# A three-step conversion of 64-bit weights with its word in an output bank, and three GpSimd tasks moved, in a fused attention and feed-forward kernel

## The chip, the core and the metric

The kernel runs on one core of a Trainium2 chip. The core has five engines with queues of their own: TensorE (PE in the profile, with its weight loads as PEld), VectorE (DVE), ScalarE (ACT), GpSimd (POOL) and SyncE (SP), which here issues almost all DMAs. Each engine takes its instructions in the order in which the program lists them, and waits where an operand is not ready. The metric is the device time of the whole program in microseconds (us), from the first to the last instruction and what lies around it; lower is better.

## What is computed

Two stages follow each other. The first is attention in 4 batches of 8 heads, with 768 tokens of 64 channels a head; a query sees only keys whose hash of six sign bits is the same. The second is a feed-forward layer on the 3072 tokens, whose two weight matrices come as 64-bit floats.

```python
q_bits = (einsum('bhsd,dk->bhsk', q, proj) > 0)      # six bits of each query
k_bits = (einsum('bhsd,dk->bhsk', k, proj) > 0)
mask = q_bucket[:, :, :, None] == k_bucket[:, :, None, :]
scores = where(mask, scale * q @ k.T, -1e9)
attn = exp(scores - max(scores)); attn = attn / (sum(attn) + 1e-9)
x = (attn @ v).transpose(0, 2, 1, 3).reshape(3072, 512)
h = x @ w_in                                          # w_in 512 x 2048, float64
g = where(h >= 1, h, where(h <= -1, 0, (h + 1)**2 / 4))
y = (g @ w_out).astype(float32)                       # w_out 2048 x 512, float64
```

## The kernel before

**Units.** The attention of the 32 heads is cut into 384 units, 12 a head: two halves of 384 queries, times six blocks of 128 keys. Here "unit 9" counts within a head; an even head and the odd head behind it share a pair of q, k and v tiles. Unit g issues two score matmuls into one of four PSUM buffers `s` (lines 372 and 373), two exponentials on ScalarE (lines 381 and 386, a rounded `ph` and an exact copy) and, one unit later, their difference `pl` on VectorE, or on GpSimd in units 0, 3, 6 and 9 (line 39 is the helper of all subtractions). Four units later come the three product matmuls with the values (lines 405, 407, 409). They gather a half of the queries in one of two output banks: bank 0 (`o_137` in the order of instructions) from unit 4 to unit 9, bank 1 (`o_138`) from unit 10 to unit 3 of the next head. When a half is complete, ScalarE copies it out (line 415).

**Row maxima.** In every second unit two matmuls `smax` (line 311) compute scores of a later head, which VectorE reduces to row maxima (line 315). There is one `smax` buffer of two banks, so the next `smax` pair can start only when the reduction of the one before is done. When all six are there, GpSimd clamps them (`max_clamp`, lines 343 and 345), TensorE transposes them (`max_tr`, line 350), ScalarE copies them (line 355) and a DMA puts them into row 7 of the operand tile `t` (line 357), which the score matmuls of that head read.

**Operands of the next pair.** GpSimd casts and splits q and k in four quarters (`cast_h`, line 153, and `low_h`) in units 0 to 3 of an even head; `move` (line 164) copies parts between partitions by DMA. `bits_mm` (line 211) computes the hash bits in an output bank that is free at that moment, ScalarE and VectorE compare them (lines 217 and 222), GpSimd scales them (line 274).

**Weights.** `WeightSplit.steps` turns a block of 128 x 512 64-bit floats into 32-bit ones by their bits. Line 69 (ScalarE) squares the high word as a float, line 70 (VectorE) shifts the high word, lines 74, 78 and 82 (VectorE) add sign, low bits, and a zero where the value is too small. Twelve blocks of `w_in` start in the odd heads 3 to 25, twelve more blocks (four of `w_in`, eight of `w_out`) in the even heads 4 to 26, and eight of `w_out` in the feed-forward stage. So from head 3 to head 26 each head has one block; its steps are set by the numbers in `conv`, units counted from the start of the head:

```python
conv((2 * i + 3) * NU, wi_steps(i, nc.scalar), (0, 7, 9, 13, 15, 17, 19, 21))
conv((4 + 2 * n) * NU, first, (0, 7, 9, 13, 15, 16))
```

The order is written by hand: `at(g, fn)` puts a task behind the matmuls of unit g, and tasks of one unit go in the order in which they were registered, weights first. On VectorE a unit reads: reduction of the last `smax`, difference `pl` of the unit before, then tasks. The feed-forward stage (`ffn`) has its own tables.

Of the kernel before, what the change touches and what calls it, by code (L numbers as in the profile page):

```python
# [22 lines left out]
P = 128  # L23
# [11 lines left out]
WMIN2 = float(np.array([897 << 20], np.int32).view(np.float32)[0]) ** 2  # L35
# [6 lines left out]
class WeightSplit:  # L42
# [3 lines left out]
    def __init__(self, nc, pool, n):  # L46
        self.nc, self.pool, self.n = nc, pool, n
        sc = pool.tile([P, 2], I32, name="wsc", bufs=1)
        nc.vector.memset(sc[:, 0:1], -0x40000000)
        nc.vector.memset(sc[:, 1:2], 29)  # L50
        self.sc = sc

    def steps(self, src, shape, hi, lo, cp, stage=None, low=None, keep=None):
# [10 lines left out]
        def s1():  # L64
            raw = st["raw"]
            sq = st["sq"] = self.pool.tile([P, n], F32, name="wsq")
            a = st["a"] = self.pool.tile([P, n], I32, name="wa", bufs=1)
            high = raw[:, :, 1].bitcast(F32)
            nc.scalar.activation(out=sq, in_=high, func=AF.Square)
            nc.vector.tensor_scalar(out=a, in0=raw[:, :, 1], scalar1=0x07FFFFFF, scalar2=3,  # L70
                                    op0=ALU.bitwise_and, op1=ALU.logical_shift_left)

        def s2():
            nc.vector.scalar_tensor_tensor(out=st["a"], in0=st["raw"][:, :, 1], scalar=self.sc[:, 0:1],
                                           in1=st["a"], op0=ALU.bitwise_and, op1=ALU.bitwise_or)

        def s3():
            nc.vector.scalar_tensor_tensor(out=st["a"], in0=st["raw"][:, :, 0], scalar=self.sc[:, 1:2],
                                           in1=st["a"], op0=ALU.logical_shift_right, op1=ALU.bitwise_or)

        def s4():
            nc.vector.scalar_tensor_tensor(out=st["sq"], in0=st["sq"], scalar=WMIN2,
                                           in1=st["a"].bitcast(F32), op0=ALU.is_ge, op1=ALU.mult)
# [13 lines left out]
        if stage is None:  # L97
            return [s0, s1, s2, s3, s4, s5, s6] + ([put] if keep is not None else [])
# [5 lines left out]
        return [s0, s1, s2, s3, s4, put], [get, s5, s6]  # L104
# [10 lines left out]
def attention(ctx, tc, wst, T1, T2, qk, v, pj, cv, x_d, s_d, e_d, tasks, shared):  # L115
# [4 lines left out]
    shared["work"], shared["small"] = work, small  # L120
# [449 lines left out]
    at(2 * NU + 1, lambda: nc.gpsimd.memset(T2[0][32:33, 0].bitcast(F32), 0.0))  # L570
    for hd in range(NH):
        pr, h = hd // 2, hd % 2
        g = hd * NU
        if 0 < hd < NH - 2:
            gc, gt = ((30, 33), (41, 43))[hd - 1] if hd < 3 else (g + NU + SHIFT - 1, g + NU + SHIFT + 1)
# [3 lines left out]
        if h == 0 and pr + 2 < NPAIR:  # L579
            g0 = g + (13, 2)[pr] if pr < 2 else g  # L580
            for n in range(4):
                at(g0 + n, cast_h, pr + 2, nc.gpsimd, n % 2, n // 2)
                at(g0 + n, low_h, pr + 2, nc.gpsimd, n % 2, n // 2)
            at(g0 + 3, move, pr + 2, 0)
            at(g0 + 3, move, pr + 2, 1)
# [3 lines left out]
            bits_at = ((20, 1), (23, 0)) if pr == 0 else ((8 if pr == 1 else 7, 1), (11, 0))  # L589
# [516 lines left out]
def lsh_attn_ffn(ctx: ExitStack, tc: tile.TileContext, qk, v, pj, cv, w_in, w_out, out):  # L1106
# [49 lines left out]

    def wi_steps(i, cp, stage=None):
        return ws.steps(win_v[:, :, i * P:(i + 1) * P, :], (P, NCT, P, 2), wih[i], wil[i], cp, stage, None, wq[i])

    def wo_steps(i, cp, stage=None, low=None):  # L1160
        return ws.steps(wout_v[i], (P, DM, 2), woh[i], wol[i], cp, stage, low)
# [3 lines left out]
    for i in range(NW1):  # L1165
        conv((2 * i + 3) * NU, wi_steps(i, nc.scalar), (0, 7, 9, 13, 15, 17, 19, 21))
    g0 = (NH - 4) * NU
    late = {}
    for n in range(NSTG):
# [8 lines left out]
        conv((4 + 2 * n) * NU, first, (0, 7, 9, 13, 15, 16))  # L1178
# [4 lines left out]
    attn = {}  # L1183
# [34 lines left out]
    for i in range(2, NFT):  # L1218
# [12 lines left out]
        else:  # L1231
            need -= 2 + (i > 9)
            *st, cast, low = wo_steps(i, nc.scalar, None, nc.vector)
            for fn, m in zip(st, (6, 4, 4, 3, 3)):
# [56 lines left out]
```

## Time and profile before

| | |
|---|---|
| time, median of 3 runs | 982.62 us (979.25, 982.62, 982.91) |
| time of the profiled execution | 979.4 us |
| its span, first to last instruction | 977.6 us |
| busy: VectorE, ScalarE, GpSimd | 788.3 us (81%), 680.2 us (70%), 354.8 us (36%) |
| granted TensorE clock | 1.00 |
| attention stage; feed-forward stage | 0 to 461 us; 461 to 977.6 us |

Spans of the profile are counted from the first instruction. The attention stage ends at 461 us with the last of the lines 405 to 409; from there on line 966, line 1061 and line 829 fill TensorE. One pair of heads (24 units) takes about 27.5 us between 82 and 384 us. Matmul ends are modelled, so a lost moment of TensorE is read from the distance of two starts rather than from its idle time: where nothing is waited for, matmuls of 384 columns start 0.17 to 0.18 us apart.

### The profile page before, as it was taken

What the parts mean: (1) busy time and instruction counts of PE and PEld (TensorE: products, weight loads), DVE (VectorE), ACT (ScalarE), POOL (GpSimd) and SP (SyncE); (2) the same over time, 40 slices, a digit from 0 to 9 for tenths busy, and PEclk for the clock granted to TensorE, in tenths of its full rate; (3) what the DMA queues carried; (4) which work ended last, traced back from release to release, by engine and by line L of the source; (5) the groups of instructions that cost most, each with busy time, mean ns of one, the idle gap of its engine ahead of it and who ended that gap; (6) DMA issues with size and microseconds to landing.
All of it is one profiled execution on the core that took longest, in us unless ns stands there. A gap on an engine that the chain in (4) does not pass through costs nothing.

```text
span 977.6 us, 15547 instructions
## 1 busy us (share of the span) xinstructions
PE 961.9 (98%) x5050; PEld 890.3 (91%) x5050; DVE 788.3 (81%) x1355; ACT 680.2 (70%) x1481; POOL 354.8 (36%) x422
## 2 busy tenths in 40 slices
PE   8999999999999999999999999999999999999998
PEld 7889999999999999999999998888988888888896
DVE  8779999999999999897898788787776777655554
ACT  7888998989989998987755565455564545544444
POOL 8768887777788877566000000000000000000000
PEclk9999999999999999999999999999999999999999
DMA  5775566677666666635494479976459554454431
GB/s 161 191 183 157 153 170 177 175 191 197 179 167 166 157 175 176 153 114 134 128 335 162 139 227 300 295 241 201 119 160 236 146 183 118 148 154 119 119 87 65
DMA packets 95113, 167.56 MB, mean 171 GB/s; under 512 B 13956, under 2 KB 51960, under 8 KB 95032
## 3 DMA queue, kind: packets, MB, share of 16 engines
q1 hardware_dynamic: 94808, 166.56, 60.7%
q8 instruction: 40, 0.66, 0.3%
q14 instruction: 41, 0.34, 0.1%
q10 hardware_dynamic: 224, 0.00, 0.0%
HBM read 106.13 MB, written 33.87 MB: 143 GB/s over the span
## 4 chain that ended last, share of the span: by engine, by line
PE 86%; DVE 5%; POOL 5%; ACT 1%; issue 1%; DMA 1%; DVEq 0%; POOLq 0%; ACTq 0%
PE y L829 27%; PE h L1061 18%; PE h L966 7%; PE smax L311 6%; PE s L373 5%; PE s L372 5%; PE o L405 5%; PE o L407 5%; PE o L409 5%; POOL t L39 3%; PE o L211 2%; DVE nm L315 2%; DVE pl L39 1%; POOL pl L39 1%; POOL t L153 1%
## 5 line engine op out<-in xcount | busy, mean ns | idle before, releaser
L381 ACT ACTIVATE ph<-s 128x384 fp32r<-128x384 f32 x380 | 188.6, 496 | 41.2 <-PE s L373 36.1
L315 DVE TENSOR_REDUCE nm<-smax 128x1 f32<-128x768 f32 x189 | 179.3, 949 | 22.2 <-PE smax L311 21.0
L39 POOL TENSOR_TENSOR pl<-pf,ph 128x384 fp32r<-128x384 f32 x128 | 134.1, 1052 | 78.8 <-ACT pf L386 78.8
L794 DVE SCALAR_TENSOR_TENSOR t<-t 128x384 f32<-128x384 f32 x128 | 71.2, 557 | 101.0 <-ACT z L789 100.8
L39 DVE TENSOR_TENSOR pl<-s,ph 128x384 fp32r<-128x384 f32 x256 | 135.4, 545 | 10.9 <-ACT s L386 9.0
L372 PE MATMUL s<-t 128*128 128x384 f32 x384 | 132.2, 344 | 0.0
L373 PE MATMUL s<-t 128*128 128x384 f32 x384 | 129.6, 337 | 1.7 <-DMA t<-te 1.7
L409 PE MATMUL o<-pl,va 128*128 128x386 f32 x384 | 130.4, 340 | 0.4 <-DVE pl L39 0.4
L407 PE MATMUL o<-ph,vb 128*128 128x386 f32 x384 | 130.0, 339 | 0.0
L405 PE MATMUL o<-ph,va 128*128 128x386 f32 x384 | 129.9, 338 | 0.0
L386 ACT ACTIVATE s<-s 128x384 f32<-128x384 f32 x252 | 125.5, 498 | 0.0
L829 PE MATMUL y<-t,ghi 128*128 128x512 f32 x384 | 124.7, 395 | 0.0
L311 PE MATMUL smax<-t 128*128 128x384 f32 x378 | 100.1, 346 | 4.5 <-DVE nm L315 4.4
L788 ACT ACTIVATE t<-h,mh 128x384 f32<-128x384 f32 x56 | 32.5, 581 | 82.2 <-PE h L966 43.5
L799 ACT CAST ghi<-z 128x384 fp32r<-128x384 f32 x129 | 65.1, 505 | 30.6 <-DVE z L795 26.9
L789 ACT ACTIVATE z<-t,m 128x384 f32<-128x384 f32 x128 | 79.0, 617 | 4.2
L829 PEld LDWEIGHTS y<-t,ghi 128*128 128x128 f32 x384 | 71.3, 188 | 11.1 <-ACT ghi L799 0.3
L1061 PE MATMUL h<-wbig,t 128*128 128x384 f32 x399 | 81.4, 336 | 0.0
L311 PEld LDWEIGHTS smax<-t 128*128 128x128 f32 x378 | 66.6, 188 | 14.5 <-DVE nm L315 13.7
L1061 PEld LDWEIGHTS h<-wbig,t 128*128 128x128 f32 x399 | 71.6, 188 | 5.2
L788 ACT ACTIVATE t<-wsq,mh 128x384 f32<-128x384 f32 x48 | 29.6, 617 | 66.7 <-DVE wsq L1074 40.4
L829 PE MATMUL y<-t,glo 128*128 128x512 f32 x192 | 76.0, 396 | 0.0
(190 smaller groups left out, 2142.9 us busy)
## 6 DMA issues: line engine op xcount, KB each, us to landing
t<-wc SPq DMA_DIRECT2D x92, 256.0 KB
t<-t SPq DMA_DIRECT2D x60, 384.0 KB
wraw<-wc SPq DMA_DIRECT2D x76, 256.0 KB
raw<-in_qk_dram SPq DMA_DIRECT2D x14, 768.0 KB
wraw<-in_w_in_dram SPq DMA_DIRECT2D x16, 512.0 KB
wraw<-in_w_out_dram SPq DMA_DIRECT2D x16, 512.0 KB
t<-ed SPq DMA_DIRECT2D x36, 192.0 KB
xd<-xs SPq DMA_DIRECT2D x32, 192.5 KB
```

The source lines that it names most:

```text
L39: eng.tensor_tensor(out=out, in0=a, in1=b, op=ALU.subtract)
L311: nc.tensor.matmul(out=smax[hd][:, hf, 0:HS], lhsT=t2[:, 0, h, i * P:(i + 1) * P], rhs=t2[:, 1, h, hf * HS:(hf + 1) * HS], start=True, sto ...
L315: nc.vector.tensor_reduce(out=nmp(hd)[:, i:i + 1], in_=smax[hd][:, :, 0:HS], axis=AX.XY, op=ALU.max, negate=True)
L372: nc.tensor.matmul(out=ps[:, 0:HS], lhsT=t1[:, 1, h, ks], rhs=t1[:, 0, h, sl], start=True, stop=False)
L373: nc.tensor.matmul(out=ps[:, 0:HS], lhsT=t2[:, 1, h, ks], rhs=t2[:, 0, h, sl], start=False, stop=True)
L381: nc.scalar.activation(out=ph[:, 0:HS], in_=ps[:, 0:HS], func=AF.Exp, scale=SCALE)
L386: nc.scalar.activation(out=pf, in_=ps[:, 0:HS], func=AF.Exp, scale=SCALE)
L405: nc.tensor.matmul(out=o, lhsT=wa, rhs=ph, start=(jj == 0), stop=False)
L407: nc.tensor.matmul(out=o, lhsT=wb, rhs=ph, start=False, stop=False)
L409: nc.tensor.matmul(out=o, lhsT=wa, rhs=pl, start=False, stop=(jj == NJ - 1))
L829: nc.tensor.matmul(out=ys[c][m], lhsT=g_[:, m * P:(m + 1) * P], rhs=w, start=(first and k == 0), stop=(last and k == 2))
L1061: nc.tensor.matmul(out=ps, lhsT=w[:, cs], rhs=x, start=(n == 0 and s not in (2, 3, 6)), stop=(n == 5), skip_group_check=True)
```

## The change

**The conversion has one VectorE step less.** ScalarE now multiplies the high word, read as a float, by 2^-112, which takes the excess of the exponent away. VectorE shifts the low word (`tail`), joins it with the product shifted by three bits (`shifted`), and then with its sign (`signed`). In the attention stage the product is written to output bank 0 (`word()`), and both joining steps read it there; in the feed-forward stage it lies in SBUF as before. `tail` and the product stand in unit 9, `shifted` in unit 12 (unit 0 of the next head), `signed` in unit 14 (its unit 2); the first product matmul in bank 0 comes in unit 16 (its unit 4).

**Bank 0 is kept free.** From pair 4 on `bits_mm` runs in units 5 and 7 of the even head, both in bank 1, where it ran in units 7 and 11 in banks 1 and 0. Comparison, `move` 3 and scaling follow.

**Three tasks at the start.** The clamp of head 3's maxima keeps unit 30 of the whole, but the last of the four casts ahead of it moves from 29 to 30, behind it; two moves go from 29 to 30, the transpose and its DMA from 33 to 32, and a memset is cut in two.

```diff
-        def s1():
-            raw = st["raw"]
-            sq = st["sq"] = self.pool.tile([P, n], F32, name="wsq")
+        def tail():
             a = st["a"] = self.pool.tile([P, n], I32, name="wa", bufs=1)
-            high = raw[:, :, 1].bitcast(F32)
-            nc.scalar.activation(out=sq, in_=high, func=AF.Square)
-            nc.vector.tensor_scalar(out=a, in0=raw[:, :, 1], scalar1=0x07FFFFFF, scalar2=3,
-                                    op0=ALU.bitwise_and, op1=ALU.logical_shift_left)
-
-        def s2():
-            nc.vector.scalar_tensor_tensor(out=st["a"], in0=st["raw"][:, :, 1], scalar=self.sc[:, 0:1],
-                                           in1=st["a"], op0=ALU.bitwise_and, op1=ALU.bitwise_or)
-
-        def s3():
-            nc.vector.scalar_tensor_tensor(out=st["a"], in0=st["raw"][:, :, 0], scalar=self.sc[:, 1:2],
-                                           in1=st["a"], op0=ALU.logical_shift_right, op1=ALU.bitwise_or)
-
-        def s4():
-            nc.vector.scalar_tensor_tensor(out=st["sq"], in0=st["sq"], scalar=WMIN2,
-                                           in1=st["a"].bitcast(F32), op0=ALU.is_ge, op1=ALU.mult)
+            nc.vector.tensor_scalar(out=a, in0=st["raw"][:, :, 0], scalar1=29, scalar2=None,
+                                    op0=ALU.logical_shift_right)
+
+        def rebias():
+            st["sq"] = self.pool.tile([P, n], F32, name="wsq")
+            g = st["g"] = st["sq"] if word is None else word()
+            nc.scalar.activation(out=g, in_=st["raw"][:, :, 1].bitcast(F32), func=AF.Copy, scale=REBIAS)
+
+        def shifted():
+            nc.vector.scalar_tensor_tensor(out=st["a"], in0=st["g"].bitcast(I32), scalar=self.sc[:, 0:1],
+                                           in1=st["a"], op0=ALU.logical_shift_left, op1=ALU.bitwise_or)
+
+        def signed():
+            nc.vector.scalar_tensor_tensor(out=st["sq"].bitcast(I32), in0=st["g"].bitcast(I32),
+                                           scalar=self.sc[:, 1:2], in1=st["a"], op0=ALU.bitwise_and,
+                                           op1=ALU.bitwise_or)
...
+    shared["work"], shared["small"], shared["word"] = work, small, lambda: obank[0]
...
-            gc, gt = ((30, 33), (41, 43))[hd - 1] if hd < 3 else (g + NU + SHIFT - 1, g + NU + SHIFT + 1)
+            gc, gt = ((30, 32), (41, 43))[hd - 1] if hd < 3 else (g + NU + SHIFT - 1, g + NU + SHIFT + 1)
...
-                at(g0 + n, cast_h, pr + 2, nc.gpsimd, n % 2, n // 2)
-                at(g0 + n, low_h, pr + 2, nc.gpsimd, n % 2, n // 2)
-            at(g0 + 3, move, pr + 2, 0)
-            at(g0 + 3, move, pr + 2, 1)
+                gq = g0 + n + (pr == 1 and n == 3)
+                at(gq, cast_h, pr + 2, nc.gpsimd, n % 2, n // 2)
+                at(gq, low_h, pr + 2, nc.gpsimd, n % 2, n // 2)
+            for n in range(2):
+                at(g0 + 3 + (pr == 1), move, pr + 2, n)
...
-            bits_at = ((20, 1), (23, 0)) if pr == 0 else ((8 if pr == 1 else 7, 1), (11, 0))
+            bits_at = (((20, 1), (23, 0)), ((8, 1), (11, 0)))[pr] if pr < 2 else ((5, 1), (7, 1))
...
-        conv((2 * i + 3) * NU, wi_steps(i, nc.scalar), (0, 7, 9, 13, 15, 17, 19, 21))
+        conv((2 * i + 3) * NU, wi_steps(i, nc.scalar), (0, 9, 9, 12, 14, 17, 19, 21))
...
-        conv((4 + 2 * n) * NU, first, (0, 7, 9, 13, 15, 16))
+        conv((4 + 2 * n) * NU, first, (0, 9, 9, 12, 14, 16))
```

**VectorE across the end of an odd head.** The rows run from the difference ahead of the step in unit 9 to the last step, in unit 15 before and 14 now. `smax` reductions are `TENSOR_REDUCE`, differences `pl<-s,ph`, weight steps write `wa` or `wsq`. Before:

```order
L39 TENSOR_TENSOR pl_167<-s,ph_160 128x384
L74 SCALAR_TENSOR_TENSOR wa<-wraw,wsc,wa 128x512
L315 TENSOR_REDUCE nm<-smax 128x1
L39 TENSOR_TENSOR pl_162<-s,ph_155 128x384
L39 TENSOR_TENSOR pl_163<-s,ph_156 128x384
L315 TENSOR_REDUCE nm<-smax 128x1
L78 SCALAR_TENSOR_TENSOR wa<-wraw,wsc,wa 128x512
L39 TENSOR_TENSOR pl_165<-s,ph_158 128x384
L315 TENSOR_REDUCE nm<-smax 128x1
L39 TENSOR_TENSOR pl_166<-s,ph_159 128x384
L82 SCALAR_TENSOR_TENSOR wsq<-wsq,wa 128x512
```

The same place in the changed kernel:

```order
L39 TENSOR_TENSOR pl_167<-s,ph_160 128x384
L66 TENSOR_SCALAR wa<-wraw 128x512
L313 TENSOR_REDUCE nm<-smax 128x1
L39 TENSOR_TENSOR pl_162<-s,ph_155 128x384
L39 TENSOR_TENSOR pl_163<-s,ph_156 128x384
L75 SCALAR_TENSOR_TENSOR wa<-o_137,wsc,wa 128x512
L313 TENSOR_REDUCE nm<-smax 128x1
L39 TENSOR_TENSOR pl_165<-s,ph_158 128x384
L79 SCALAR_TENSOR_TENSOR wsq<-o_137,wsc,wa 128x512
L313 TENSOR_REDUCE nm<-smax 128x1
L39 TENSOR_TENSOR pl_166<-s,ph_159 128x384
```

The middle step has moved from behind the second reduction of the piece to ahead of it, the last step from behind the third to ahead of it.

**GpSimd in units 28 to 30 of the whole.** `t_0_77` and `t_0_74` are operand tiles of a later pair, `nm` holds the maxima of head 3. Before, from the third cast on:

```order
L153 CAST t_0_77<-raw 128x384
L39 TENSOR_TENSOR t_0_74<-raw,t_0_77 128x384
L153 CAST t_0_77<-raw 128x384
L39 TENSOR_TENSOR t_0_74<-raw,t_0_77 128x384
L343 TENSOR_SCALAR nm<-nm 128x6
L345 TENSOR_SCALAR nm<-nm 128x6
L39 TENSOR_TENSOR pl_164<-pf,ph_157 128x384
```

And in the changed kernel:

```order
L151 CAST t_0_77<-raw 128x384
L39 TENSOR_TENSOR t_0_74<-raw,t_0_77 128x384
L341 TENSOR_SCALAR nm<-nm 128x6
L343 TENSOR_SCALAR nm<-nm 128x6
L151 CAST t_0_77<-raw 128x384
L39 TENSOR_TENSOR t_0_74<-raw,t_0_77 128x384
L39 TENSOR_TENSOR pl_164<-pf,ph_157 128x384
```

The two clamps now stand ahead of the fourth cast and its difference.

**SyncE's queue behind them.** `t_1_78<-te` is the DMA of head 3's maxima into row 7, the copies between `t_0` tiles are `move`. Before:

```order
L164 DMA t_0_77<-t_0_77 64x1536
L164 DMA t_0_74<-t_0_77 64x1536
L164 DMA t_0_74<-t_0_74 64x1536
L357 DMA t_1_78<-te 1x6x128
L358 DMA ed_67<-te 6x128
```

And in the changed kernel:

```order
L162 DMA t_0_77<-t_0_77 64x1536
L162 DMA t_0_74<-t_0_77 64x1536
L355 DMA t_1_78<-te 1x6x128
L356 DMA ed_67<-te 6x128
L162 DMA t_0_74<-t_0_74 64x1536
```

The DMA of the maxima has passed the third `move`.

More of the change, by code (lines that the diff above doesn't have):

```diff
@@ L97, in steps @@
         if stage is None:
-            return [s0, s1, s2, s3, s4, s5, s6] + ([put] if keep is not None else [])
+            return [s0, tail, rebias, shifted, signed, s5, s6] + ([put] if keep is not None else [])
         def get(sq=None):
@@ L102, in get @@
             nc.sync.dma_start(out=st["sq"], in_=stage)
-        return [s0, s1, s2, s3, s4, put], [get, s5, s6]
+        return [s0, tail, rebias, shifted, signed, put], [get, s5, s6]
 NQK, NV, NP_ = 3, 2, 7
```

22 lines of the change are left out of this document (12 added, 10 removed).

## The prediction

> **What bounds the kernel now.** I read the page's first part, then busy time by stages, then the waits, then the order of time around single waits.
>
> ```profile
> PE 961.9 (98%) x5050; PEld 890.3 (91%) x5050; DVE 788.3 (81%) x1355; ACT 680.2 (70%) x1481; POOL 354.8 (36%) x422
> 82.00:430.00 348.00, 344.94 (x1941) 334.76 (x1940) 323.98 (x483) 315.52 (x757) 269.18 (x296) 1.00 0.66 172
> 461.00:977.60 516.60, 512.28 (x2545) 459.50 (x2544) 371.21 (x718) 273.97 (x517) 2.54 (x2) 1.00 0.59 175
> ```
>
> The last two rows are stages: bounds, length, then busy time of PE, PEld, DVE, ACT and POOL. TensorE is the bound in both. In the feed-forward stage it lacks 4.3 us, and VectorE is busy for 371 of 517 us, so the eight blocks converted there are not on the path: I cost them at nothing, hidden behind TensorE. In the attention stage VectorE is busy for 93% of the time. So VectorE time is worth only what it takes out of TensorE's waits. These are, in the same stretch (total, times, longest):
>
> ```profile
> PEld smax L311 <- DVE nm L315: 6.8, 19, 0.7
> PEld s L350 <- POOL nm L345: 4.3, 8, 0.6
> PE s L350 <- POOL nm L345: 1.8, 8, 0.3
> ```
>
> There are two kinds: `smax` waits for the reduction ahead of it, the transpose waits for GpSimd's clamp. One wait of the first kind:
>
> ```profile
> 216.32 0.34 PE L409 MATMUL o<-pl,va 128*128 128x386 f32 x1
> 216.66 0.62 PE L311 MATMUL smax<-t 128*128 128x384 f32 x2
> 217.11 0.35 PE L372 MATMUL s<-t 128*128 128x384 f32 x1
> 213.72 0.55 DVE L39 TENSOR_TENSOR pl<-s,ph 128x384 fp32r<-128x384 f32 x1
> 214.18 1.55 DVE L74 SCALAR_TENSOR_TENSOR wa<-wraw,wsc,wa 128x512 int32<-128x512 int32 x1
> 215.66 0.95 DVE L315 TENSOR_REDUCE nm<-smax 128x1 f32<-128x768 f32 x1
> 216.52 1.01 DVE L39 TENSOR_TENSOR pl<-s,ph 128x384 fp32r<-128x384 f32 x2
> 217.45 0.94 DVE L315 TENSOR_REDUCE nm<-smax 128x1 f32<-128x768 f32 x1
> 218.87 0.51 PE L311 MATMUL smax<-t 128*128 128x384 f32 x2
> ...
> 77.88 0.63 PE L311 MATMUL smax<-t 128*128 128x384 f32 x2 [0.49 <-DVE nm L315]
> 163.80 0.62 PE L311 MATMUL smax<-t 128*128 128x384 f32 x2 [0.42 <-DVE nm L315]
> ```
>
> A matmul normally starts 0.175 us after the one before. `smax` starts 0.34 after line 409, and the next matmul 0.45 after the pair instead of 0.35: 0.26 us lost. The reduction ends at 216.61, and TensorE starts 0.05 later. What made it late is line 74, 1.55 us long. Counted by starts, 11 of the 19 waits are of this place and size (unit 0 of an even head, 2.9 us); four of 0.24 stand at 90 us and behind the three batch sums (1.0 us), three of 0.79 at the batch sums themselves (163.80 is the first, idle for 0.42 by its row, 0.79 by the starts around it); the last is small. The first weight block, ahead of this stretch, loses 0.75 by starts at 77.88.
>
> **The change part by part.** *VectorE's work.* Durations, as shortest, median, longest:
>
> ```profile
> L70 DVE TENSOR_SCALAR wa<-wraw x32: 416/424/1190, 73.1 to 536.0; 128x512 int32<-128x512 int32 x32
> L74 DVE SCALAR_TENSOR_TENSOR wa<-wraw,wsc,wa x32: 729/754/1572, 75.4 to 536.5; 128x512 int32<-128x512 int32 x32
> L82 DVE SCALAR_TENSOR_TENSOR wsq<-wsq,wa x32: 673/691/1253, 82.1 to 540.4; 128x512 f32<-128x512 f32 x32
> L39 DVE TENSOR_TENSOR pl<-s,ph x256: 486/545/560, 14.7 to 459.5; 128x384 fp32r<-128x384 f32 x128
> ```
>
> Before, a block costs lines 70, 74, 78, 82. After, it costs one like line 70 and two that read PSUM and SBUF. No such one of 512 columns is in the trace. Below it is bounded by the 384-column difference, 0.55; above by line 82 at its longest, 1.25. I take 0.68, since line 82 at its shortest has the length, and the difference, which also reads one operand in PSUM, never exceeds 0.56 in 256 cases. Two instructions overlap by about 0.07, so the pitch is 0.61.
>
> *The wait in unit 0 (`smax` at 216.66).* `tail` stands where line 74 stood. That one was long because a GpSimd subtraction began just ahead of it:
>
> ```profile
> 214.16 1.02 POOL L39 TENSOR_TENSOR pl<-pf,ph 128x384 fp32r<-128x384 f32 x1 [2.33 <-ACT pf L386]
> 218.69 1.34 POOL L39 TENSOR_TENSOR t<-raw,t 128x384 fp32r<-128x384 f32 x1
> 221.54 0.68 POOL L343 TENSOR_SCALAR nm<-nm 128x6 f32<-128x6 f32 x1
> 222.30 0.23 POOL L345 TENSOR_SCALAR nm<-nm 128x6 f32<-128x6 f32 x1
> 222.59 0.28 PE L350 MATMUL s<-ident,nm 128*12 128x128 f32 x1 [0.23 <-POOL nm L345]
> ```
>
> Both starts follow from TensorE's and stay. So I give `tail` the long form of line 70, 1.19 instead of 1.55, a gain of 0.36 (at most 1.13, if it comes at 0.42). The 0.16 and the 0.10 behind it go: **-2.9 us** over 11 places, and -0.35 at the first block. The four of 0.24 lie where line 70 stood in unit 7, which is empty now: **-1.0 us**.
>
> *A new wait in unit 2.* `shifted` now stands ahead of the reduction that began at 217.45, where line 78 stood behind it. That reduction starts 0.36 earlier and 0.61 later, at 217.70, and releases TensorE at 218.70. The next `smax`, at 218.87 now, will be ready 0.26 earlier, at 218.61. It is 0.09 late, and with the 0.10 behind any such wait it loses 0.2: 8 places, **+1.6 us** (bounds: 0 if `tail` is short, 0.8 a place if `shifted` takes 1.25). At the three batch sums this wait is there already, 0.79 long; it grows by the same two amounts, the reduction 0.25 later and TensorE 0.26 earlier, 0.5 each: **+1.5 us**.
>
> *The same in unit 2 of odd heads.* The same order stands there, but no wait does now. The second group of `bits_mm` used to lie ahead of it (four matmuls, 0.70 us in which VectorE could catch up) and has gone to unit 7, and the comparison with it. I take half of the other boundary, 0.1 at 12 places: **+1.2 us**, between 0 and 3.1 (0.26 each).
>
> *The product on ScalarE.* It replaces a square of the same shape, 0.65 us (below), in unit 9 instead of 7, behind the copy of bank 0. Nothing waits for it but `shifted`, three units later: nothing. *The lock on bank 0:* behind the reduction at 217.70 and a difference, `signed` runs from 219.04 to 219.72; the first product matmul of unit 4 is the ninth behind the `smax` at 218.61, at 220.19. All of TensorE is queued behind that matmul, but 0.45 us are left.
>
> *`bits_mm` in units 5 and 7 of one bank.* The second group waits for the comparison of the first:
>
> ```profile
> 224.80 0.86 PE L211 MATMUL o<-t,pw 128*128 128x384 f32 x4
> 225.60 0.65 ACT L69 ACTIVATE wsq<-wraw 128x512 f32<-128x512 f32 x1
> 226.27 0.48 ACT L217 ACTIVATE neg<-o 32x384 f32<-32x384 f32 x1
> 226.78 0.55 DVE L222 TENSOR_TENSOR neg<-o,neg 32x384 f32<-32x384 f32 x1 [0.47 <-ACT neg L217]
> 223.07 1.02 POOL L39 TENSOR_TENSOR t<-raw,t 128x384 fp32r<-128x384 f32 x1
> ```
>
> From the start of the group to the end of the comparison are 2.53 us now, 0.65 of it a square that goes. In the changed order 16 matmuls lie between the two starts, 2.8 us. So no wait for it. The last split that the second group reads ends at 224.09, and the group would begin near 225.2. At nothing, then; without the square's going 0.3 us would be left. `move` 3 and the scaling come earlier and hold up nobody with a due date; the half-unit memsets lie ahead of a cast that waits for its data anyway.
>
> *The transpose in unit 5.* GpSimd runs without a break from 214.16 to the clamp at 222.53; the chain of waits leads back along it. The split at 218.69 is 0.32 over the 1.02 of others; line 78 follows the reduction at 217.45, so it begins just ahead of it. The clamp at 221.54 is 0.45 over its 0.23; by VectorE's order line 82 runs there, one reduction and two differences later. Neither instruction is there then, and two that read PSUM stand in their place. The transpose loses 0.35 to 0.42 at 8 places; the clamp comes up to 0.77 earlier while TensorE gains about 0.1. I take all: **-3.0 us** (other bound 0).
>
> *Head 3's maxima at the start.*
>
> ```profile
> 55.96 0.51 POOL L153 CAST t<-raw 128x384 fp32r<-128x384 f32 x1
> 57.53 0.23 POOL L343 TENSOR_SCALAR nm<-nm 128x6 f32<-128x6 f32 x1
> 57.32 0.86 PE L211 MATMUL o<-t,pw 128*128 128x384 f32 x4
> 58.90 0.27 PE L350 MATMUL s<-ident,nm 128*12 128x128 f32 x1
> 56.49 2.42 SPq L164 DMA_DIRECT2D t<-t  x3
> 60.12 0.76 SPq L357 DMA_DIRECT2D t<-te  x1
> 63.85 0.44 PE L373 MATMUL s<-t 128*128 128x384 f32 x1 [1.70 <-DMA t<-te]
> ```
>
> The clamp takes the cast's place at 55.96 and ends at about 56.5. The transpose goes ahead of line 211, at 57.32. SyncE has two moves ahead of the DMA; the first waits for the last cast, now done near 57.0, and three took 2.42 to issue. So the DMA goes out at about 58.3, 1.8 us earlier, which covers the 1.70: **-1.75 us**, counted by starts; 0 if something else ends last there. The move it passes is late by its issue, 0.8 us, and belongs to a later pair.
>
> **Sum:** -2.9 - 0.35 - 1.0 + 1.6 + 1.5 + 1.2 - 3.0 - 1.75 = **-4.7 us**. The profiled execution took 979.4 us (977.6 and 1.8 around it), so the sum gives 974.7; from the median, 982.62, it gives 977.9. Of four executions of the kernel before, two lie at 979 and two at 983, so I name a value between: **976.5 us**.
>
> **The rivals.** *No new waits (972.2).* If `tail` comes at 0.42, or the two joining steps nearer to 0.55, the waits in unit 2 vanish: 4.3 us less. For it: half of line 70's 32 instances take at most 424 ns, though GpSimd is busy for 77% of this stage. Against it: the two starts at 214.16 and 214.18 are tied to the same matmuls.
>
> *The joining steps are held up by GpSimd (989.9).* If they behave as line 82 does, `shifted` takes 1.25, and the reduction behind it comes 0.56 later: at 24 boundaries 13.4 us, -4.7 + 13.4 = +8.7, slower. It decides from 0.2 us a boundary on. Against it stand the 256 differences, 486 to 560 ns, many beside GpSimd work. [...]
>
> *One of the two GpSimd gains fails (979.5 or 978.3).* If the clamps stay late, 3.0 us are missing; if another transfer ends last at 63.85, 1.75.
>
> [...]
>
> ```profile
> L803 DVE TENSOR_TENSOR glo<-z,ghi 128x384 fp32r<-128x384 f32 x128 | 70.3, 549 | 0.2 <-ACT ghi L799 0.2
> ```
>
> This one reads SBUF alone, at the same size as the difference's 545.
>
> **How the numbers follow.** The forecast has 0.56, no new waits 0.17, the held-up steps 0.09, a failing GpSimd gain 0.18. A measurement of this kernel tells about 0.5%, 4.9 us, from no change. The forecast lies on that edge: half of it is faster (0.28), half the same. With 0.17 and 0.01, faster is 0.46; slower is 0.08; the same is 0.46. The range takes in the first rival from the lower base and no gain from the upper: 969.5 to 983.
>
> **What would show it.** Right: line 74's place holds an instruction near 1.2 us; no wait of line 373 near 62 us; no waits of the transpose for the clamp; waits of `smax` short, and in unit 2. Wrong: joining steps over 0.8 us, matmuls of line 405 that wait for `signed`, matmuls of `bits_mm` that wait for the comparison, or a time over 983.

## The result and the profile after

The changed kernel takes 995.01 us (median of 5 runs, 993.0 to 996.37), the kernel before on the same chip 979.25 (5 runs, 978.84 to 982.91). The ratio is 1.0146, with a 95% interval from 1.0128 to 1.0164: 1.5% slower, where 976.5 us and a range up to 983 had been named. The profiled execution has a span of 992.8 us, 15.2 more than before.

The first line of the page for the changed kernel, busy time by engine:

```profile
PE 964.8 (97%) x5050; PEld 889.5 (90%) x5050; DVE 780.0 (79%) x1323; ACT 681.9 (69%) x1481; POOL 321.3 (32%) x423
```

VectorE is busy for 8 us less (a held-up `tail` counts in it whole, 2.64 to 2.67 us each; line 66 adds up to 48.5), GpSimd for 34 us less, and TensorE has the same 5,050 matmuls. So nothing here is more work; the 15 us are waits. TensorE's waits in the whole kernel (total, times, longest), the first three lines:

```profile
PE smax L309 <- DVE nm L313: 16.9, 24, 1.2
PE smax L424 <- DVE idle L469: 1.3, 1, 1.3
PE s L371 <- DMA t<-te: 1.2, 1, 1.2
```

The transposes' waits for GpSimd's clamp are gone; the waits of `smax` for the reduction have come instead, up to 1.2 us long. One of them, first TensorE's rows, then VectorE's, then GpSimd's (start, duration, engine, line):

```profile
210.10 0.62 PE L309 MATMUL smax<-t 128*128 128x384 f32 x2 [1.22 <-DVE nm L313]
212.55 0.62 PE L309 MATMUL smax<-t 128*128 128x384 f32 x2
...
206.05 0.54 DVE L39 TENSOR_TENSOR pl<-s,ph 128x384 fp32r<-128x384 f32 x1
206.51 2.66 DVE L66 TENSOR_SCALAR wa<-wraw 128x512 int32<-128x512 int32 x1
209.10 0.95 DVE L313 TENSOR_REDUCE nm<-smax 128x1 f32<-128x768 f32 x1
...
205.97 0.97 POOL L272 TENSOR_SCALAR bits<-neg,cvt 32x768 fp32r<-32x768 f32 x1
206.92 1.00 POOL L39 TENSOR_TENSOR vb<-vraw,va 128x384 fp32r<-128x384 f32 x1
207.89 1.00 POOL L39 TENSOR_TENSOR pl<-pf,ph 128x384 fp32r<-128x384 f32 x1
209.79 1.00 POOL L39 TENSOR_TENSOR pl<-pf,ph 128x384 fp32r<-128x384 f32 x1 [0.90 <-ACT pf L384]
```

Line 66 is `tail`, in unit 9 of an even head. It begins while GpSimd scales the bits (line 272), and ends 0.28 us after GpSimd's third instruction from there; the reduction behind it ends at 210.05, and TensorE starts at 210.10. It has lost 1.38 us by the distance of the starts, and 0.11 behind the pair. The durations of the three steps over the whole kernel (shortest, median, longest in ns):

```profile
L66 DVE TENSOR_SCALAR wa<-wraw x32: 418/1266/2667, 74.7 to 551.4; 128x512 int32<-128x512 int32 x32
L75 DVE SCALAR_TENSOR_TENSOR wa<-o,wsc,wa x24: 735/741/745, 78.6 to 413.6; 128x512 int32<-128x512 int32 x24
L79 DVE SCALAR_TENSOR_TENSOR wsq<-o,wsc,wa x24: 734/742/745, 80.7 to 415.6; 128x512 int32<-128x512 int32 x24
```

`tail` has three lengths by its place: 0.42 in the 8 blocks of the feed-forward stage, 1.26 in the 12 odd heads, and 2.64 to 2.67 in 11 of 12 even heads (0.80 in the other). The 48 joining steps of the attention stage never leave 0.734 to 0.745.

By the starts of matmuls, TensorE's losses in the attention stage, before and after, and the term of the sum:

| place | before | after | change | predicted |
|---|---|---|---|---|
| `smax`, unit 0 of even heads, 11 | 2.8 | 0 | -2.8 | -2.9 |
| `smax` of the first block | 0.76 | 0.47 | -0.3 | -0.35 |
| `smax`, four of 0.24 | 1.0 | 0 | -1.0 | -1.0 |
| `smax`, unit 2 of even heads, 8 | 0 | 2.75 | +2.75 | +1.6 |
| `smax` at the batch sums, 3 | 2.4 | 2.2 | -0.2 | +1.5 |
| `smax`, unit 2 of odd heads, 12 | 0 | 4.15 | +4.15 | +1.2 |
| transposes for the clamp, 8 | 3.1 | 0 | -3.1 | -3.0 |
| head 3's maxima, 63.85 | 1.85 | 1.36 | -0.5 | -1.75 |
| `smax`, unit 0 of odd heads, 11 | 0 | 16.1 | **+16.1** | not seen |

The changes add up to 15.1 us; the spans differ by 15.2. One row makes the result.

### The profile page after: what moved, and what is told of

Same layout as the page of the kernel before. It is cut to its first block, busy times and chain, and to the rows that moved or that the text cites. A ratio compares the mean times of both kernels' runs of the same rounds, so it can differ in the third digit from the quotient of the medians.

```text
span 992.8 us, 15529 instructions
## 1 busy us (share of the span) xinstructions
PE 964.8 (97%) x5050; PEld 889.5 (90%) x5050; DVE 780.0 (79%) x1323; ACT 681.9 (69%) x1481; POOL 321.3 (32%) x423
## 4 chain that ended last, share of the span: by engine, by line
PE 70%; DVE 19%; ACT 5%; issue 3%; DMA 1%; POOL 0%; SPq 0%; DVEq 0%; POOLq 0%; ACTq 0%
PE y L829 26%; PE h L1061 18%; PE h L966 7%; DVE nm L313 6%; DVE pl L39 5%; PE smax L309 5%; DVE wa L66 3%; PE s L371 3%; PE s L370 3%; PE o L407 3%; PE o L403 3%; PE o L405 3%; ACT ph L379 2%; DVE wa L75 2%; ACT s L384 1%
## 5 line engine op out<-in xcount | busy, mean ns | idle before, releaser
L39 POOL TENSOR_TENSOR pl<-pf,ph 128x384 fp32r<-128x384 f32 x128 | 130.6, 1021 | 90.4 <-ACT pf L384 90.3
L829 PE MATMUL y<-woh,glo 128*128 128x512 f32 x192 | 75.7, 394 | 0.2
```

The lines of the kernel that those rows point to most:

```text
L39: eng.tensor_tensor(out=out, in0=a, in1=b, op=ALU.subtract)
L829: nc.tensor.matmul(out=ys[c][m], lhsT=g_[:, m * P:(m + 1) * P], rhs=w, start=(first and k == 0), stop=(last and k == 2))
```

## The experiments

Times stand beside the kernel before on the same chip; "caught" is an instruction of about 2.5 us or more in unit 9 of an even head, 12 places in a run.

**First: undo one thing each.** In the changed kernel, `tail` back to unit 7 (e1); the scaling of the bits back to unit 13 (e2).

```diff
 e1
-        conv((2 * i + 3) * NU, wi_steps(i, nc.scalar), (0, 9, 9, 12, 14, 17, 19, 21))
+        conv((2 * i + 3) * NU, wi_steps(i, nc.scalar), (0, 7, 9, 12, 14, 17, 19, 21))
...
-        conv((4 + 2 * n) * NU, first, (0, 9, 9, 12, 14, 16))
+        conv((4 + 2 * n) * NU, first, (0, 7, 9, 12, 14, 16))
 e2
-            at(g + n + (2 if pr else 1), bits_scale, pr + 2, nc.gpsimd if pr else nc.scalar)
+            at(g + (13 if pr > 1 else n + (2 if pr else 1)), bits_scale, pr + 2, nc.gpsimd if pr else nc.scalar)
```

> The changed kernel with one thing undone: the first step of the weight words (tail, a shift of one input, SBUF to SBUF) stands in unit 7 again, where the kernel before had its first step of the same form. Theory A (VectorE's one-input shift cannot start while GpSimd runs instructions back to back; in unit 9 of even heads that run is three long): in unit 7 the shift takes 0.42 to 0.5 us nearly everywhere, the 11 waits of smax of 1.35 us in unit 0 of odd heads go (15 us), the short ones in unit 2 stay: about 980 us, between 977 and 983. Theory B (it is the product's word in PSUM, the joining steps, or the moved comparison of the bits that cost the time): the waits stay, about 995 us.

> The changed kernel with one thing undone: the scaling of the bits on GpSimd stands in unit 13 of even heads again instead of unit 9, so that beside tail GpSimd runs two instructions back to back and not three. Theory A: tail in unit 9 of even heads takes what is left of the two, between 0.8 us (if it gets in between them) and 1.8, instead of 2.66; the 11 waits of 1.35 us shrink to 0.5 or less: 981 to 986 us. Theory A2 (one GpSimd instruction beside it is enough, the run's length does not matter) and theory B (word, joining steps): 992 to 996 us.

e1 took 979.24 us against 981.04, ratio 0.9977 (0.9965 to 0.999); e2 980.15, ratio 0.999 (0.998 to 0.9999). `tail` over the whole kernel in e1:

```profile
L66 DVE TENSOR_SCALAR wa<-wraw x32: 418/508/906, 71.3 to 533.9; 128x512 int32<-128x512 int32 x32
```

and in e2:

```profile
L66 DVE TENSOR_SCALAR wa<-wraw x32: 418/722/1271, 75.9 to 536.9; 128x512 int32<-128x512 int32 x32
```

Either undoing takes the 15 us away, so theory B falls: the word in PSUM and the joining steps stay in both. In e2 `tail` still begins in the middle of a GpSimd instruction with another queued directly behind it, yet takes 0.70 to 0.73 in even heads: it is let in at the end of the first. So a run of GpSimd instructions without a gap is not enough to hold it up, as theory A had it.

**Second: the form of the step.** `tail` at its place with two inputs (e3).

```diff
...
+        nc.vector.memset(sc[:, 2:3], 0)
...
+        nc.vector.memset(self.by, 29)
...
-            nc.vector.tensor_scalar(out=a, in0=st["raw"][:, :, 0], scalar1=29, scalar2=None,
-                                    op0=ALU.logical_shift_right)
+            nc.vector.scalar_tensor_tensor(out=a, in0=st["raw"][:, :, 0], scalar=self.by[:, 0:1],
+                                           in1=self.sc[:, 2:3].to_broadcast([P, n]),
+                                           op0=ALU.logical_shift_right, op1=ALU.bitwise_or)
```

> The changed kernel with tail at the same place, doing the same shift, but as an instruction with two inputs (the second a column of zeros, spread). Theory A, form matters: a two-input step gets in at the next end of a GpSimd instruction, as line 74 of the kernel before did (0.73 to 0.88 in even heads, 1.55 in odd heads); in even heads about 1.0 us instead of 2.66, in odd heads 1.55 instead of 1.26, so the 15 us go and about 2.9 come: about 983 us. Rival (the place decides: any VectorE instruction that reads SBUF is held up there): 2.6 us as now, about 995 us.

1002.33 us, ratio 1.022 (1.0205 to 1.0236), caught in 12 of 12:

```profile
L69 DVE SCALAR_TENSOR_TENSOR wa<-wraw,wby,wsc x32: 743/1527/2946, 76.6 to 561.4; 128x512 int32<-128x512 int32 x32
```

My theory A fell here: the form with two inputs is caught as well, and being longer costs more. What remains is the GpSimd side, the scaling.

**Third: what stands in the run.** The scaling in unit 9 replaced by a third difference on 128 partitions (e5), spread to 128 partitions (e6), replaced by a product of two inputs of 384 columns on the same 32 (e7, which leaves out the scaling and the second half of the bits, so that its output is not the kernel's; it serves for the time of the step alone). e6 is also run with 32 (e13, its control) and 64 partitions (e14).

```diff
 e5 (with the scaling in unit 13 as in e2)
...
+            if pr > 1:
+                at(g + 9, split_v, pr + 1, nc.gpsimd, 0)
 e6 (e13, e14: 32 and 64 in place of P)
-    cvt = const.tile([32, 2], F32, name="cvt")
+    cvt_all = const.tile([P, 2], F32, name="cvt")
+    cvt = cvt_all[0:32]
+    bt_all = small.tile([P, S], F32R, name="bits", bufs=1)
+    neg_all = small.tile([P, S], F32, name="neg", bufs=1)
+    nc.gpsimd.memset(cvt_all, 0.0)
+    nc.gpsimd.memset(neg_all, 0.0)
...
-        eng.tensor_scalar(out=bt, in0=neg, scalar1=cvt[:, 0:1], scalar2=cvt[:, 1:2],
+        eng.tensor_scalar(out=bt, in0=neg_all, scalar1=cvt_all[:, 0:1], scalar2=cvt_all[:, 1:2],
 e7
...
-        eng.tensor_scalar(out=bt, in0=neg, scalar1=cvt[:, 0:1], scalar2=cvt[:, 1:2],
-                          op0=ALU.mult, op1=ALU.add)
+        eng.tensor_tensor(out=bt[:, 0:HS], in0=neg[:, 0:HS], in1=neg[:, HS:S], op=ALU.mult)
```

> The changed kernel with the scaling of the bits back in unit 13 of even heads, and in its place in unit 9 a second copy of the split of v (a difference of 128x384, the same length of 1.0 us, written twice with the same values). GpSimd runs three long instructions back to back beside tail again, but the middle one is a difference with two inputs on 128 partitions. Theory L (the length of the run starves tail): tail takes 2.6 us in even heads, some 992 to 996 us. Theory K (it is what stands in the run, the scaling with one input on 32 partitions, at whose end VectorE does not get in): tail gets in at the next end, 0.7 us as without it, about 981 us.

> The changed kernel with the scaling of the bits in unit 9 as it is, one input and 768 columns, but over 128 partitions instead of 32 (the rows added are zeros that nobody reads). Theory K1 (32 partitions make the difference): tail gets in at the end of the scaling, 0.7 to 1.0 us in even heads, about 982 us. Theory K2 (the form with one input makes it) and theory L (length): 2.6 us, 992 to 996 us.

> The changed kernel with the scaling of the bits in unit 9 replaced by a product of two inputs of 384 columns on the same 32 partitions (the scaling and the second half of the bits are left out). Theory K1 (32 partitions): tail still takes 2.6 us in even heads, 992 to 996 us. Theory K2 (the form with one input): 0.7 to 1.0 us, about 982 us. Theory L (length): 2.6 us.

> The control to the run with the scaling on 128 partitions: the changed kernel with the same edit (fixed tiles of their own for the bits, cleared at the start) but on 32 partitions. Theory K1 (the number of partitions was what counted there): tail in unit 9 of even heads takes 2.66 us in nearly all of 12 places, about 995 us. Rival (the new place of the tiles or the start did it): 0.7 us, about 980 us.

> The same edit with the scaling on 64 partitions. Theory K1 in its strict form (any scaling on fewer than all 128 partitions): 2.66 us in most places, 990 to 996 us. If the misses belong to 32 partitions or fewer: 0.7 us, about 980 us. Both can come in one run, as in the run with the product on 32 partitions.

In e6, the same place as above (VectorE, then GpSimd):

```profile
201.70 0.73 DVE L66 TENSOR_SCALAR wa<-wraw 128x512 int32<-128x512 int32 x1
202.36 0.95 DVE L317 TENSOR_REDUCE nm<-smax 128x1 f32<-128x768 f32 x1
...
201.15 1.00 POOL L276 TENSOR_SCALAR bits<-neg,cvt 128x768 fp32r<-128x768 f32 x1
202.10 1.20 POOL L39 TENSOR_TENSOR vb<-vraw,va 128x384 fp32r<-128x384 f32 x1
203.25 1.02 POOL L39 TENSOR_TENSOR pl<-pf,ph 128x384 fp32r<-128x384 f32 x1
```

`tail` ends 0.28 us after the scaling, and now it is the difference behind it that is longer, 1.20. The scaling itself costs the same: 0.986 us at the median on 128 partitions, 0.975 on 32. e6 took 979.84 us, e5 977.43 and e7 981.82 (one execution each, beside 979.85); the control e13 took 993.56 and e14 997.63 (two each, 980.26 before, ratios 1.012 and 1.016).

**Fourth: that part of the change alone**, on the kernel before with its old four steps, the scaling on 32 partitions (e9) and on 128 (e15, with the edit of e6).

```diff
-            bits_at = ((20, 1), (23, 0)) if pr == 0 else ((8 if pr == 1 else 7, 1), (11, 0))
+            bits_at = (((20, 1), (23, 0)), ((8, 1), (11, 0)))[pr] if pr < 2 else ((5, 1), (7, 1))
```

> The kernel before with one part of the change alone: the two groups of bits_mm in units 5 and 7, both in bank 1, and with them the scaling of the bits on GpSimd in unit 9 instead of 13; the weight words are the old four steps. Theory K (a long instruction on 32 partitions at whose end VectorE is not let in, whatever its step): line 74 in unit 9 of even heads, 0.73 us before, is caught like tail and takes some 2.9 us in most places, so this part alone costs about 15 us less the 3 us of the transposes' waits: 988 to 994 us. Rival (line 74 stands a little ahead of the scaling, or as the runs with other instructions there it gets in after it): 0.73 to 1.5 us, no waits of the transposes for the clamp, 975 to 979 us.

> The kernel before with the bits' groups and the scaling moved alone (ninth run, 999.4 us, line 74 at 2.55 us in 12 of 12 even heads), with the scaling on 128 partitions. Theory K1: line 74 is let in at the end of the scaling, 0.6 to 0.9 us, the 12 waits of 1.6 us go: 976 to 981 us. Rival (line 74's form of two inputs is missed anyway, since it starts only 0.05 us ahead of that end): 2.55 us, about 999 us.

e9 took 999.36 us, ratio 1.020 (1.0176 to 1.0224), some 5 us more than expected: by starts the 12 waits of `smax` in unit 0 of odd heads cost 20.3 us, and the transposes' waits stayed. e15 took 980.99, ratio 1.0008 (0.9989 to 1.0027). Line 74 and GpSimd in e9, then in e15:

```profile
209.50 2.57 DVE L74 SCALAR_TENSOR_TENSOR wa<-wraw,wsc,wa 128x512 int32<-128x512 int32 x1
...
208.60 0.97 POOL L274 TENSOR_SCALAR bits<-neg,cvt 32x768 fp32r<-32x768 f32 x1
209.55 1.01 POOL L39 TENSOR_TENSOR vb<-vraw,va 128x384 fp32r<-128x384 f32 x1
210.52 1.00 POOL L39 TENSOR_TENSOR pl<-pf,ph 128x384 fp32r<-128x384 f32 x1
```

```profile
229.40 0.73 DVE L74 SCALAR_TENSOR_TENSOR wa<-wraw,wsc,wa 128x512 int32<-128x512 int32 x1
...
228.48 0.99 POOL L278 TENSOR_SCALAR bits<-neg,cvt 128x768 fp32r<-128x768 f32 x1
229.44 1.57 POOL L39 TENSOR_TENSOR vb<-vraw,va 128x384 fp32r<-128x384 f32 x1
230.97 1.01 POOL L39 TENSOR_TENSOR pl<-pf,ph 128x384 fp32r<-128x384 f32 x1
```

Apart from the fixed tiles, with which the step is caught on 32 partitions too (e13), one thing differs, the number of partitions of the scaling, and the VectorE step takes 2.57 or 0.73. So moving the bits and their scaling alone makes the kernel slower, with none of the new weight words in it. All runs together:

| run | GpSimd's instruction as the step begins | step | caught |
|---|---|---|---|
| changed kernel | scaling, 32 partitions | one input | 11 of 12 |
| e13 | the same, fixed tiles | one input | 10 of 12 |
| e14 | scaling, 64 | one input | 12 of 12 |
| e3 | scaling, 32 | two inputs | 12 of 12 |
| e9 | scaling, 32 | line 74, two inputs | 12 of 12 |
| e7 | product of two inputs, 32 | one input | 1 of 12 |
| e6 | scaling, 128 | one input | 0 of 12 |
| e15 | scaling, 128 | line 74, two inputs | 0 of 12 |
| e2, e5 | difference, 128 | one input | 0 of 24 |

In all these places another GpSimd instruction is queued directly behind. A run made for another term, e11 below, has the scaling on 32 partitions with nothing behind it for 1.5 us, and a step with two SBUF inputs (`signed`) beginning half-way through it:

```profile
207.05 1.00 DVE L79 SCALAR_TENSOR_TENSOR wsq<-wsq,wsc,wa 128x512 int32<-128x512 int32 x1
...
206.53 0.97 POOL L272 TENSOR_SCALAR bits<-neg,cvt 32x768 fp32r<-32x768 f32 x1
209.00 0.23 POOL L341 TENSOR_SCALAR nm<-nm 128x6 f32<-128x6 f32 x1 [1.49 <-DVE nm L313]
```

There it takes 0.97 to 1.02 us at 12 of 12 places: it is let in at the end of the scaling. As far as this one place shows, both belong to the catch: the scaling on few partitions and a GpSimd instruction queued behind it.

**Fifth: other cuts and terms of the sum.** e4 cuts the three steps so that none has one input in SBUF: the shift of the word from PSUM in unit 11, the low bits joined in 13, the sign in 14.

```diff
...
+            nc.vector.tensor_scalar(out=a, in0=st["g"].bitcast(I32), scalar1=3, scalar2=None,
+                                    op0=ALU.logical_shift_left)
...
+            nc.vector.scalar_tensor_tensor(out=st["a"], in0=st["raw"][:, :, 0], scalar=self.sc[:, 0:1],
+                                           in1=st["a"], op0=ALU.logical_shift_right, op1=ALU.bitwise_or)
```

> The changed kernel with another cut of the same three steps, none of which has one input in SBUF: the product by ScalarE in unit 9, then the shift of the word in PSUM in unit 11, the low bits joined to it in unit 13 (as line 78 of the kernel before), the sign in unit 14. Theory A: no step is starved, unit 9 of even heads loses its 15 us; what stays are short waits of 0.1 to 0.3 behind the steps in units 11 and 13: about 979 us, between 975 and 983. Theory B (the word in PSUM costs it): as the changed kernel, 992 to 996 us, since it is read from PSUM twice as there.

985.27 us, ratio 1.0047 (1.003 to 1.0064): between the two. Nothing is caught, but the product matmuls of line 403 start late in unit 4 of 24 heads, 5.1 us in all by starts (one place, 0.54, in e1), and those of line 405 behind them 1.8 us. This is the lock on bank 0, held longer since the sign comes behind the low bits: at all 24 places line 403 starts 0.145 to 0.147 us after the end of `signed`, though the profile names other releasers for some of these waits. The transposes wait again as well, 0.19 us at 8 places.

e10 is e1 with the word in SBUF, so that the joining steps read two inputs from there (`word=None`); e11 is e10 with the bits' groups where the kernel before has them. Not shown are `tail` in unit 7, as in e1, and the same edit for `w_out`.

```diff
 e10
...
-        return ws.steps(win_v[:, :, i * P:(i + 1) * P, :], (P, NCT, P, 2), wih[i], wil[i], cp, stage, None, wq[i], word)
+        return ws.steps(win_v[:, :, i * P:(i + 1) * P, :], (P, NCT, P, 2), wih[i], wil[i], cp, stage, None, wq[i])
 e11
...
-            bits_at = (((20, 1), (23, 0)), ((8, 1), (11, 0)))[pr] if pr < 2 else ((5, 1), (7, 1))
+            bits_at = (((20, 1), (23, 0)), ((8, 1), (11, 0)))[pr] if pr < 2 else ((7, 1), (11, 0))
```

> The first run (tail in unit 7) with the word in SBUF: ScalarE writes the product into the block's own tile, and the two joining steps read two inputs from SBUF. [...] If steps with two inputs in SBUF are held up by GpSimd and those from PSUM are not, the joining steps take 0.75 to 1.5 us in attention and the waits in unit 2 of odd or even heads grow: 981 to 990 us.

> The run with the word in SBUF, with the bits' two groups where the kernel before has them (unit 7 in bank 1, unit 11 in bank 0, scaling in unit 13), which the word in an output bank does not allow. It tests one term of the prediction: that the waits of smax in unit 2 of odd heads come because the second group of bits_mm, 0.70 us of TensorE ahead of that place, has gone. If so, these 11 or 12 waits of 0.36 us go (4 us) while those of the same unit of even heads stay, and some 3 us of the transposes' waits may come back: the same time or 1 to 2 us less than the run it is compared with. If not, both kinds stay and the time is 0 to 3 us more.

e10 took 983.28 us, ratio 1.0035 (1.0017 to 1.0054), e11 983.72, ratio 1.0029 (1.0014 to 1.0044). Two rows of e10, TensorE's largest wait and the first joining step:

```profile
PE s L348 <- POOL nm L343: 6.2, 13, 0.6
...
L75 DVE SCALAR_TENSOR_TENSOR wa<-wsq,wsc,wa x32: 739/744/1289, 79.6 to 540.9; 128x512 int32<-128x512 int32 x32
```

At the median the joining step is as long from SBUF (744 ns) as from PSUM (741). What differs is GpSimd: a difference beside a joining step takes 1.26 to 1.58 instead of 1.02 in 34 of 36 cases, its clamp comes late again, and the transposes' waits return, 0.63 us by starts at 12 places where the kernel before had 0.39 at 8. In e11 the 12 waits of `smax` in unit 2 of odd heads, 0.22 each and 2.6 us in all in e10, are gone, and those in unit 2 of even heads stay (3.4 us in both). Two units later, in unit 4 of odd heads, e11 has new ones of 0.16: there the reduction stands behind the `signed` shown above, which takes 1.00 beside the scaling and not 0.74.

e8 is e1 with the first joining step in unit 11; e12 is e8 with the DMA of head 3's maxima ahead of two copies on SyncE's queue.

```diff
 e8
-        conv((2 * i + 3) * NU, wi_steps(i, nc.scalar), (0, 7, 9, 12, 14, 17, 19, 21))
+        conv((2 * i + 3) * NU, wi_steps(i, nc.scalar), (0, 7, 9, 11, 14, 17, 19, 21))
...
-        conv((4 + 2 * n) * NU, first, (0, 9, 9, 12, 14, 16))
+        conv((4 + 2 * n) * NU, first, (0, 7, 9, 11, 14, 16))
 e12
...
-                at(g0 + 3 + (pr == 1), move, pr + 2, n)
+                at(32 if pr == 1 else g0 + 3, move, pr + 2, n)
```

> The changed kernel with tail in unit 7 (as the first run) and the first joining step (shifted) in unit 11 instead of 12, so that it stands two instructions earlier and ahead of a place where VectorE waits for a smax, no longer directly ahead of the reduction that TensorE waits for in unit 2. Theory (after the first run what is left in the attention stage are the 20 waits of about 0.36 us in unit 2 that the step in unit 12 makes): they go or shrink to 0.1, 972 to 977 us. Rival (VectorE has no room in unit 11 either, the wait only moves): 978 to 980 us.

> The eighth run (tail in unit 7, first joining step in unit 11) with one change more: at the start, the DMA of head 3's maxima goes ahead of the two copies between operand tiles that SyncE issued before it (0.52 and 0.59 us, waiting for the last early cast). Theory (its lateness is the queue: it left at 59.24 while its data were ready at 58.13): it leaves near 58.1 and the stall of 1.40 us at the first score matmul of head 3 shrinks to about 0.3, so 1.1 us less, about 972.4 us. Rival (the flight of 4.4 us is the DMA engines busy with other transfers, and takes as much longer as it leaves earlier): the stall stays above 1 us, 973.5 us.

**e8 beats both kernels**: 973.55 us against 979.85, ratio 0.993 (0.9912 to 0.9948). The waits of `smax` in the attention stage, 9.6 us by starts in e1 and 26.2 in the changed kernel, are 3.0 there, in 8 places instead of 25 and 36 (counted where `smax` starts late; behind 19 other pairs e8 loses another 1.9 us). The transposes' waits come back in part, 0.16 to 0.19 us at 7 places. e12 took 976.54, ratio 0.9962 (0.9947 to 0.9977), no better than e8. The stall of head 3 is not in its trace, which its edit need not have done (it is not in e1 and e5 either), and these two rows came instead, the first weight block and the `smax` behind it, 1.65 us late by starts:

```profile
73.51 0.43 DVE L66 TENSOR_SCALAR wa<-wraw 128x512 int32<-128x512 int32 x1 [1.94 <-DMA wraw<-in_w_in_dram]
...
75.32 0.61 PE L309 MATMUL smax<-t 128*128 128x384 f32 x2 [1.50 <-DVE nm L313]
```

The block's load stands behind the copies on the same queue and left 0.7 us later than in e8; VectorE, in order, stood at `tail` until it came.

## Why the prediction was wrong

**The step that failed** is "So I give `tail` the long form of line 70, 1.19", together with "`move` 3 and the scaling come earlier and hold up nobody with a due date". The first was worked out at one place, 214.18 in an odd head, and there it was right: 1.26 us, and the 11 waits of 0.26 are gone. It was then used for all of unit 9. In even heads line 74 had taken 0.73 to 0.88, beside two differences of GpSimd and no scaling, and I looked at neither that place nor at the neighbour that the second sentence sends there. The place before the change:

```profile
228.59 0.73 DVE L74 SCALAR_TENSOR_TENSOR wa<-wraw,wsc,wa 128x512 int32<-128x512 int32 x1
...
227.52 2.68 POOL L39 TENSOR_TENSOR vb<-vraw,va 128x384 fp32r<-128x384 f32 x2
```

The scaling has no due date itself; what mattered is which VectorE step begins beside it. The runs showed 2.64 to 2.67 us there in place of 1.19, and the price was +16.1 us, not in the sum at all. e2 and e9 show it from both sides: the scaling put back takes it away, the bits and the scaling moved alone bring it. e15 shows that the scaling on 32 partitions is what counts in that move.

**The rival that ended slower** had the right resource and the wrong step. The joining steps, which it expected at 1.25, were never held up (0.734 to 0.745). For `tail` I had counted on a wait for the one GpSimd instruction under way, by the long form of line 70; the trace agrees for odd heads (0.98 us of a difference and 0.28) and not for even ones, where it waited for the rest of the scaling (0.43 us at 206.51) and two instructions more (until 208.89).

**Terms that held:** the waits of unit 0 in even heads, the first block, the four of 0.24, and the transposes (-3.1 against -3.0). For the last the mechanism is shown by e10, where steps with two SBUF inputs bring the waits back (0.63 us at 12 places), and by e9, where the bits are moved, the old steps stay and the eight waits stay at 3.1 us. That all of it was gained is in part luck: in e8 TensorE loses 0.1 in place of 0.35 in unit 2 of most even heads, and at 7 of the 8 places the transpose waits again, 1.2 us in all. At the eighth, head 12, TensorE loses 0.45 in unit 2, and there is no such wait.

**Terms that were mis-sized.** The joining step is 0.74 and not 0.68. The waits in unit 2 are 0.35 at each of 20 places, 6.9 us where 2.8 were counted. For odd heads the reason was right, the size was not: with the second group of `bits_mm` back in its place (e11) the waits of this unit go, as was argued; but "half of the other boundary" had no ground, since without the group odd and even heads lose the same. The batch sums did not get longer (-0.2 instead of +1.5). Without the caught step these terms leave about -1.0 us of the -4.7, and e1, the changed kernel without the caught step (`tail` in unit 7), measures -1.8.

**Head 3's maxima:** the stall fell by 0.5 instead of 1.75. The DMA left 1.38 us earlier, at 58.74, and not 1.8:

```profile
57.49 1.16 SPq L162 DMA_DIRECT2D t<-t  x2
58.74 1.21 SPq L355 DMA_DIRECT2D t<-te  x1
63.15 0.44 PE L371 MATMUL s<-t 128*128 128x384 f32 x1 [1.20 <-DMA t<-te]
```

From its issue to the matmul are 4.41 us, 3.73 before. The chain begins earlier than the prediction looked, at the first of the four casts, which waits for the load of q and k:

```profile
50.37 0.50 POOL L153 CAST t<-raw 128x384 fp32r<-128x384 f32 x1 [0.29 <-DMA raw<-in_qk_dram]
...
50.85 0.50 POOL L151 CAST t<-raw 128x384 fp32r<-128x384 f32 x1 [1.42 <-DMA raw<-in_qk_dram]
```

The first row is the kernel before, the second the changed one. From the start of this cast to the matmul that waits are 13.48 us before (13.49 in e9, 13.51 in e15), and 12.27 to 12.32 in the changed kernel and in the nine of its variants that have the wait. So the new order is worth 1.2 us and not 1.75. The DMA does leave 1.86 earlier as counted from the cast, but it now goes out directly behind the moves, where its issue takes 1.21 us instead of 0.76. The other 0.7 us are when the load landed and when TensorE came, not the change: the cast waited from 0.06 us (e1, e5, without the stall) to 2.58 (e2, with 1.40) in runs whose code is the same up to there. Why the load lands so differently is open.

## What to carry to other kernels

When an instruction is moved on GpSimd, list the VectorE steps with SBUF operands that begin beside its new place, in every kind of iteration, and measure that pair before trusting the sum: beside a difference on 128 partitions the step here waited for one GpSimd instruction (1.26 us in odd heads of the changed kernel), beside the scaling on 32 for the whole run of three (2.64 to 2.67 in even ones). A step's length taken from one kind of iteration said nothing of the other here, and the prediction's own row for line 74, 729 to 1572 ns, held both kinds, 0.73 in even heads and 1.55 in odd. In SyncE's queue, which works in order, an earlier place for one task was a later one for the next, and what is late there may be the path: in e12 the load of the first block left 0.7 us later, and the `smax` behind it came 1.65 late.

## What the runs showed of the hardware

In the changed kernel, e3, e9, e13 and e14 a VectorE step on SBUF operands began during the scaling (one input, 0.97 us on 32 partitions) on 32 or 64 partitions, with another GpSimd instruction queued directly behind. In 57 of 60 places it was not let in at the scaling's end, nor at the end of the next instruction, and came in when GpSimd's run of three was over: it took 2.66 us at 206.51 of the changed kernel, 2.57 in e9, at most 2.69 in e14 and 2.95 in e3. A run of more than three was not tried. With nothing queued behind, it came in at the end of the scaling at 12 of 12 (e11, 0.97 to 1.02 us). The same scaling on 128 partitions took as long (0.99 us), and the step was let in at its end at 24 of 24 with the next instruction queued (0.73 us in the rows of e6 and e15). So the changed kernel was mended without moving anything, by clearing and scaling rows that nobody reads (e6, 979.84 us, one execution). With a product of two inputs on 32 partitions (e7) 1 of 12 was caught, so the number of partitions is not all of it. The start of the step did not tell the two kinds apart: `tail` began 0.53 to 0.57 us into the scaling where it was caught, 0.55 to 0.58 where it was not, line 74 0.91 to 0.93 and 0.90 to 0.94. What in GpSimd makes the difference was not found.
